# Wider token slots, smaller weight units and one issue order in a fused attention and gated feed-forward kernel

## The chip, the cores and the metric

The kernel runs on one core of a Trainium2 chip. The time is device microseconds from start to end of one execution; 0.5% of it (3.7 us) is about what can be told from no change. Engines: PE (TensorE, matmuls; PEld its weight loads), DVE (VectorE), ACT (ScalarE), POOL (GpSimd) and SP, whose queue issues every DMA. Each engine works its own instructions off in order and waits on semaphores for the others.

## What is computed

```python
# q, k, v: 8 batches x 8 heads x 576 tokens x 64; phi: ... x 32 memories
a = softmax(phi)                                  # over the 32 memories
k_m, v_m = einsum('bhsm,bhsd->bhmd', a, k), einsum('bhsm,bhsd->bhmd', a, v)
attn = softmax(q @ k_m.T / 8)                     # 576 x 32 a head
x = (attn @ v_m) laid out as (4608 tokens, 512)
h = x @ w_in                                      # 512 -> 2048, weights in float64
g = h * clip(h + 3, 0, 6) / 6
out = (g @ w_out).astype(float32)                 # 2048 -> 512, weights in float64
```

## The kernel before

**Folding.** Since x = attn @ v_m, the kernel multiplies v_m into w_in for each batch (the fold, `fold`, L376) and takes the probabilities times that product: h = attn @ (v_m @ w_in). Probabilities, folded weights, gated values and w_out are each split into a high and a low part, and each product is made of three matmuls (high-high, low-high, high-low). The float64 weights arrive as pairs of 32-bit words, and ACT and DVE turn them into float32 in units of 1024 columns (magnitude, rounding, clamp, shift, sign, total); w_in is then kept in DRAM (`w_kept`) and read back for every later batch.

**Slots.** The work after the fold goes in slots: batch b, one block f of 128 of the 2048 hidden columns, and 256 (hf 0) or 320 (hf 1) tokens. A slot is a first GEMM of six matmuls (`gemm1`, L409) into one of two PSUM buffers `ph`, a relu of h + 3 on ACT (L419), a gate on DVE (L423), a high half on ACT (L440), a low half on DVE (L444), and a second GEMM of 2 token tiles x 3 matmuls of 512 columns (`gemm2`, L455) that adds up over all 16 f in a PSUM bank for each token tile. The last 64 tokens of each batch go to a tile `rest`, and two batches' make slots of their own (hf 2). At the end of a run of slots the banks are scaled and stored (`leave`, `store`).

**PSUM.** Four banks for the second GEMM's sums, two for `ph`, and one pair of banks (`psum`, tag pa) that memories, turn, scores and fold take in turn. Each fold makes 512 columns and is drained in two steps of 256 (`folded_high` on ACT, `folded_low` on DVE, L392).

**Attention of a batch.** For batches 0 and 1 the maxima of phi are spread over the partitions by a matmul. From batch 2 on they go through DRAM: `maxima` on DVE from `ptile` (L236), `maxima_out` (L241) writes them to DRAM tensor nmx four bytes at a time, and `spread` (L246) reads them back to every partition as nmxb; then `less_max` on DVE (L261, in three parts), `phi_exp`, `memories` on PE, `turn`, `scores`, and the softmax: transpose, maximum, subtraction on POOL, exponential, sum, division on POOL, transpose back, split. `ptile` and the queries `qh` share a ring of two buffers (`WIDE`).

**Order.** It is written out by hand: BEGIN lists every step word by word up to batch 2, and STEADY says after which slot of a batch each step for the next comes. `play` issues the words in turn, so each engine's queue has its steps in the order of the words. In STEADY the maxima of batch b + 2 come at slot 22 of batch b, their spread at slot 28, and the subtractions with the first slots of the batch after; scores come at slots 8 and 10, and the softmax is spread up to slot 18.

**The words.** pt, pn, kv, q: loads; mx, mo, sp: maxima, their write, their spread; xa, xe: `less_max`, `phi_exp`; kvm, nr, nk, tp, tk: memories up to turned; sc, ct, cm, cs, ex, ds, dr, dm, bt, bh, bl: scores to split probabilities; fo, vh, vl: fold and its two drains; ab, ro, cl, sh, si, to: conversion; g, u, m, k, h, l, a: a slot's first GEMM, relu, gate, rest, high, low, second GEMM; e, eo: `leave`, `store`; fetch, wk: w_in units from and to DRAM.

Of the kernel before, what the change touches and what calls it, by code (L numbers as in the profile page):

```python
# [22 lines left out]
W = (2 * P, S - 2 * P)  # L23
OFF = (0, 2 * P)
REST = S - 4 * P
# [3 lines left out]
NCHUNK = 4  # L29
FC = DF // NCHUNK  # L30
FPC = FC // P
UNIT = 2 * FC
KV = 2 * D + 1
EPS = 1e-9
LAG = 3
VC = 256
VW_RING = {"tag": "vw", "bufs": 6}
TMP = {"tag": "tmp", "bufs": 2}
O_RING = {"tag": "o", "bufs": 2}
# [6 lines left out]

PARTS = ((0, 2), (2, 4), (4, 5))

BEGIN = """
pt.0 raw.0.0 raw.0.1 pn.0 raw.0.2 raw.0.3 kv.0.0 kv.0.1 kv.0.2 mx.0 kv.0.3 md.0 me.0 kv.0.4 ab.0.0.0 ro.0.0.0  # L50
cl.0.0.0 q.0.0 xa.0.0 xa.0.1 xe.0.0 raw2.0 xa.0.2 xe.0.1 sh.0.0.0 xe.0.2 q.0.1 si.0.0.0 ab.0.0.1 ro.0.0.1
raw2.1 cl.0.0.1 kvm.0.0 sh.0.0.1 kvm.0.1 to.0.0.0 kvm.0.2 si.0.0.1 kvm.0.3 kvm.0.4 nr.0 to.0.0.1 nk.0 tp.0 tk.0
sc.0.0 ab.1.0 pt.1 ct.0.0 pn.1 kv.1.0 kv.1.1 kv.1.2 kv.1.3 cm.0.0 fo.0.0 ro.1.0 cl.1.0 kv.1.4 sc.0.1 cs.0.0
sh.1.0 warm.4 ex.0.0 vh.0.0.0 ds.0.0 vh.0.0.1 wk.0 dr.0.0 ab.1.1 dm.0.0 ro.1.1 bt.0.0 q.1.0 mx.1 bh.0.0 raw2.2
ct.0.1 md.1 cm.0.1 q.1.1 me.1 warm.3 vl.0.0.0 cs.0.1 xa.1.0 raw2.3 vl.0.0.1 xe.1.0 xa.1.1 ex.0.1 kvm.1.0 xe.1.1
ds.0.1 kvm.1.1 raw.1.0 si.1.0 kvm.1.2 raw.1.1 xa.1.2 cl.1.1 kvm.1.3 raw.1.2 xe.1.2 dr.0.1 kvm.1.4 sh.1.1 dm.0.1
nr.1 raw.1.3 si.1.1 nk.1 tp.1 raw2.4 tk.1 bl.0.0 sc.1.0 bt.0.1 g.0 ct.1.0 bh.0.1 g.1 to.1.0 raw2.5 u.0 bl.0.1
# [32 lines left out]
bt.2.0 mo.3 ds.2.1 a.56 bh.2.0 m.58 bl.2.0 l.57 h.58 g.60 l.58 u.59 a.57 m.59 u.60 dr.2.1 h.59 m.60 dm.2.1 k.59  # L90
fo.2.0 l.59 h.60 l.60 g.61 bt.2.1 vh.2.0.0 a.58 bh.2.1 vl.2.0.0 vh.2.0.1 bl.2.1 g.62 u.61 vl.2.0.1 a.59 u.62
m.61 m.62 h.61 k.61 l.61 h.62 g.63 l.62 a.60 u.63 m.63 sp.3 q.3.1 h.63 fetch.2.2 a.61 h.64 l.63 k.63 l.64 a.62
h.65 l.65 a.63 e0.62 h.66 e1.62 a.64 l.66 eo.62 h.67 e0.63 e1.63 h.68 a.65 l.67 l.68 h.69 a.66 eo.63 l.69 h.70
a.67 l.70 h.71 a.68 l.71
"""

STEADY = """
0 fold.C.1 un.C.1.0 / 1 un.C.1.1 exps.N.0 / 2 exps.N.1 / 3 exps.N.2 / 5 mem.N / 6 norm.N / 7 turn.N / 8 score.N.0
/ 9 centre.N.0 / 10 exp.N.0 score.N.1 / 11 div.N.0 pt.M / 12 centre.N.1 pn.M / 13 fold.C.2 un.C.2.0 back.N.0 kvs.M
# [7 lines left out]
def attention_ffn_kernel(ctx: ExitStack, tc: tile.TileContext, pn, pt, kv, qt, w1, w2, out):  # L107
# [591 lines left out]
```

## Time and profile before

| | us |
|---|---|
| three runs, median (lowest to highest) | 746.48 (744.11 to 747.0) |
| profiled execution, span from first to last instruction | 744.8 |
| PE busy, of the span | 707.8 (95%) |
| DVE busy | 443.6 (60%) |
| ACT busy | 367.1 (49%) |
| POOL busy | 79.3 (11%) |

The own time of the profiled execution is not given, only its span. Busy shares are means over stages that differ; the slices and windows below show them apart. A busy PE is one with a matmul under way, and matmuls overlap, so the pace is read from the starts of successive groups, not from the length of one.

### The profile page before, as it was taken

The numbers are of one execution on the slowest core, as the hardware profiler recorded it, in microseconds if no ns is written. First come the engines' busy times: TensorE is split into PE (matmuls) and PEld (weight loads), VectorE is DVE, ScalarE is ACT, GpSimd is POOL, SyncE is SP. The second block draws the span as 40 slices with busy tenths as digits, with TensorE's granted clock in tenths as the row PEclk, the third lists the DMA queues.
The fourth block names the chain that finished last, engine by engine and source line by source line (L and its number), as shares of the span: only waits on it lengthen the run. The fifth ranks groups of instructions, "written<-read, shape, count | busy, mean of one in ns | idle before, by whom it ended". The sixth has DMA issues, their size and how long they took to land.

```text
span 744.8 us, 12219 instructions
## 1 busy us (share of the span) xinstructions
PE 707.8 (95%) x4706; PEld 566.8 (76%) x4706; DVE 443.6 (60%) x963; ACT 367.1 (49%) x801; POOL 79.3 (11%) x59
## 2 busy tenths in 40 slices
PE   2859999997999999999999999999999999999997
PEld 1337877875878887888888788788887888888885
DVE  5799999984674464546544465456644465454442
ACT  4457777652454354445444454454443454444442
POOL 0044111120120030003000020002100021000000
PEclk9979999999999999999999999999999999999999
DMA  9991825059940442337251362519081211130002
GB/s 318 370 415 64 292 104 209 1 57 315 367 179 15 186 152 16 141 112 282 8 149 57 111 241 10 147 58 323 15 156 58 73 56 57 58 114 1 1 1 70
DMA packets 26042, 99.77 MB, mean 134 GB/s; under 512 B 4224, under 2 KB 4992, under 8 KB 21376
## 3 DMA queue, kind: packets, MB, share of 16 engines
q1 hardware_dynamic: 25984, 98.99, 41.3%
q8 instruction: 37, 0.61, 0.3%
q14 instruction: 21, 0.17, 0.1%
HBM read 83.25 MB, written 15.73 MB: 133 GB/s over the span
## 4 chain that ended last, share of the span: by engine, by line
PE 81%; DMA 8%; DVE 5%; ACT 3%; issue 3%; SPq 0%; ACTq 0%; DVEq 0%
PE acc L455 49%; PE ph L409 25%; PE pv L376 4%; PE pk L273 2%; DMA ptile<-in_pt 2%; DMA qh<-in_qt 2%; DMA kvt<-in_kv 2%; DMA o<-partial 2%; PE psc L311 1%; ACT gf L419 1%; DVE glo L444 1%; DVE gf L423 1%; DVE pnat L261 1%; DMA raw<-in_w 1%; DVE tmp L161 0%
## 5 line engine op out<-in xcount | busy, mean ns | idle before, releaser
L455 PE MATMUL acc<-w,ghi 128*128 128x512 f32 x1152 | 325.8, 401 | 2.0 <-DVE o L482 1.3
L455 PEld LDWEIGHTS acc<-w,ghi 128*128 128x128 f32 x1152 | 202.8, 189 | 61.1 <-issue 16.4
L419 ACT ACTIVATE gf<-ph,three 128x256 f32<-128x256 f32 (+1 forms) x256 | 127.5, 500 | 166.9 <-PE ph L409 159.0
L423 DVE SCALAR_TENSOR_TENSOR gf<-gf,ph 128x256 f32<-128x256 f32 (+1 forms) x256 | 109.1, 427 | 151.9 <-ACT gf L419 150.7
L409 PEld LDWEIGHTS ph<-phi,both 128*128 128x128 f32 x1024 | 164.7, 190 | 39.0 <-DVE gf L423 12.8
L409 PE MATMUL ph<-phi,both 128*128 128x320 f32 (+1 forms) x1024 | 182.9, 301 | 7.1 <-DVE gf L423 6.7
L455 PE MATMUL acc<-w,glo 128*128 128x512 f32 x576 | 185.2, 397 | 0.0
L440 ACT CAST ghi<-gf 128x256 fp32r<-128x256 f32 x256 | 103.7, 406 | 116.5 <-DVE gf L423 116.3
L444 DVE TENSOR_TENSOR glo<-gf,ghi 128x256 fp32r<-128x256 f32 x256 | 119.8, 470 | 49.9 <-ACT ghi L440 49.5
L455 PEld LDWEIGHTS acc<-w,glo 128*128 128x128 f32 x576 | 108.7, 189 | 25.7 <-DVE glo L444 0.3
L409 PE MATMUL ph<-plo,both 128*128 128x256 f32 (+1 forms) x512 | 110.2, 297 | 0.0
L409 PEld LDWEIGHTS ph<-plo,both 128*128 128x128 f32 x512 | 82.9, 190 | 0.0
L392 DVE TENSOR_TENSOR both<-pv,both 128x512 fp32r<-128x512 f32 x64 | 44.0, 689 | 43.7 <-ACT both L387 43.6
L342 POOL TENSOR_TENSOR st<-st,mx 128x640 f32<-128x640 f32 (+1 forms) x15 | 18.6, 1238 | 372.7 <-DVE mx L338 372.7
L387 ACT CAST both<-pv 128x512 fp32r<-128x512 f32 x64 | 37.1, 583 | 2.6 <-PE pv L376 2.0
L376 PE MATMUL pv<-w,kvT 64*32 64x512 f32 x512 | 36.0, 619 | 0.9 <-DVE st L327 0.9
L273 PE MATMUL pk<-kvt,pnat 128*32 128x129 f32 (+1 forms) x640 | 23.9, 293 | 11.8 <-DMA kvt<-in_kv 8.8
L273 PEld LDWEIGHTS pk<-kvt,pnat 128*32 128x32 f32 (+1 forms) x640 | 17.5, 115 | 18.8 <-ACT raw L149 6.4
L183 POOL TENSOR_TENSOR w<-tmp,w 128x1024 fp32r<-128x1024 f32 x8 | 19.7, 2460 | 81.2 <-ACT w L179 42.4
L367 POOL TENSOR_TENSOR plo<-pT,phi 128x640 fp32r<-128x640 f32 (+1 forms) x15 | 22.4, 1494 | 39.2 <-ACT phi L362 39.2
L354 POOL TENSOR_TENSOR st<-st,sm 128x640 f32<-128x640 f32 (+1 forms) x15 | 18.0, 1202 | 47.6 <-DVE sm L350 47.6
L444 DVE TENSOR_TENSOR glo<-rest,ghi 128x256 fp32r<-128x256 f32 x32 | 13.5, 422 | 15.8 <-PE acc L455 15.8
(56 smaller groups left out, 360.0 us busy)
## 6 DMA issues: line engine op xcount, KB each, us to landing
w<-w_kept SPq DMA_DIRECT2D x24, 1024.0 KB, 8.4
kvt<-in_kv SPq DMA_DIRECT2D x32, 516.0 KB, 8.6
raw<-in_w SPq DMA_DIRECT2D x16, 512.0 KB, 8.7
raw<-in_w SPq DMA_DIRECT2D x8, 1024.0 KB, 14.0
out_t<-o SPq DMA_DIRECT2D x16, 512.0 KB, 2.8
pnat<-in_pn SPq DMA_DIRECT2D x8, 640.0 KB, 6.0
qh<-in_qt SPq DMA_DIRECT2D x8, 640.0 KB, 10.1
ptile<-in_pt SPq DMA_DIRECT2D x8, 576.0 KB, 4.0
```

Of the source, the lines that this page charges most:

```text
L183: nc.gpsimd.tensor_tensor(w2_sb[u][:, 1], whole, w2_sb[u][:, 0].bitcast(F32), ALU.subtract)
L273: nc.tensor.matmul(self.pk[j * M : (j + 1) * M, g, :KV], self.pnat[:rows, t, g * P + j * M : g * P + (j + 1) * M], kvt[:rows, g * NJ + j, ...
L367: self.aux[hf].tensor_tensor(plo, self.pT[hf], probs[self.b, hf][0].bitcast(F32), ALU.subtract)
L376: nc.tensor.matmul(self.pv[c][j * M : (j + 1) * M, g, :], self.kvT[rows, g, j * M : (j + 1) * M], chunk[rows, j, :].bitcast(F32), start=Tr ...
L387: nc.scalar.copy(both[:, 0], self.pv[c][:, :, VC * k : VC * (k + 1)])
L392: nc.vector.tensor_tensor(both[:, 1], src, both[:, 0].bitcast(F32), ALU.subtract)
L409: nc.tensor.matmul(self.ph, w[:, g, fs], x[:, g * n : (g + 1) * n], start=(i == 0), stop=(i == len(seq) - 1),)
L419: nc.scalar.activation(self.gf, self.ph, AF.Relu, bias=three)
L423: nc.vector.scalar_tensor_tensor(gf[:, :n], gf[:, :n], 6.0, ph[:, :n], ALU.min, ALU.mult)
L440: nc.scalar.copy(self.ghi, self.gated())
L444: nc.vector.tensor_tensor(self.glo, self.gated(), self.ghi.bitcast(F32), ALU.subtract)
L455: nc.tensor.matmul(accs[self.b, self.hf][0 if one else k], (self.glo if i == 2 else self.ghi)[:, k * P : (k + 1) * P], w2lo if i == 1 else ...
```

## The change

- Slots take all 576 tokens of a batch for one f: `gemm1` makes 2 x 6 matmuls of 288 columns into a pair of banks, relu and gate are one instruction each over both, the high and low halves take 512 columns, and `gemm2` makes 4 tiles x 3 matmuls. There are 128 slots, 32 for batches 0 and 1 (numbered 0 to 31), then 16 for each batch (96 to 111 are batch 6's).
- The second GEMM of a slot may be issued in quarters (a.95.0 is token tile 0 of slot 95).
- The `ph` buffers and the single pair are replaced by a ring of two pairs (`two_banks`) that first GEMMs, memories, turn, scores and folds share.
- Units of w_in are 256 columns. One word folds one unit, two, or four in a row (two units share a pair of banks); from batch 2 on it is four.
- The halves of scores and softmax are 288 tokens each; the gate of the last 64 tokens goes by way of ACT (`gate_rest`) for every batch; those of two batches make four groups of four f (rh, rl, ra: high, low, second GEMM).
- Loads of batch 1 go to room that later holds parts of w_out. Temporaries, halves and outputs share one ring of six pages.
- BEGIN and STEADY are replaced by ORDER, one list of 1816 words for all engines. `maxima_out` and `spread` are unchanged.

The core of the diff (one stretch of ORDER is shown, from the last slots of batch 5 to the first of batch 6):

```diff
-W = (2 * P, S - 2 * P)
-VC = 256
+HALF = S // 2
+MAIN = 4 * P
+UC = 256
+UNIT = NJ * UC
+PAGE = {"tag": "page", "bufs": 6}
 WIDE = {"tag": "wide", "bufs": 2}
+RUNS = ((0, 0, 6, "keep"), (1, 0, 8, "keep"), (0, 6, 16, "add"), (1, 8, 16, "add"))
...
+ORDER = """
...
+fetch.6.0 k.92 l.90 u.93 m.93 g.94 kv.7.0 k.90 k.93 u.94 h.93 l.93 g.95 a.90 u.95 m.94 m.95 sc.6.0 sc.6.1 a.91 rh.2.1
+h.94 pt.7 ct.6.1 ct.6.0 cm.6.0 fo.6.0.1.2.3 cm.6.1 a.92 a.93 fetch.6.7 cs.6.1 cs.6.0 ex.6.1 mx.7 vh.6.0 ex.6.0 mo.7
+ds.6.1 dr.6.1 q.7.1 vh.6.1 dm.6.1 ds.6.0 fetch.6.4 bt.6.1 sp.7 vh.6.3 dr.6.0 rh.2.2 l.94 h.95 vh.6.2 dm.6.0 l.95 k.95
+a.94 xa.7.0 bh.6.1 kv.7.1 bt.6.0 bh.6.0 xa.7.2 a.95.0 bl.6.1 a.95.1 vl.6.2 rl.2.1 fetch.6.6 a.95.2 fetch.6.5 vl.6.0
+vl.6.1 bl.6.0 rl.2.2 e.7.1 k.94 g.96 a.95.3 vl.6.3 g.97 rh.2.3 u.97 m.97 e.7.3 k.97 u.96 m.96 ra.2.0 g.98 e.7.0 g.99
...
-    ps_h = ctx.enter_context(tc.tile_pool(name="ps_h", bufs=2, space=bass.MemoryType.PSUM))
-    ps_a = ctx.enter_context(tc.tile_pool(name="ps_a", bufs=1, space=bass.MemoryType.PSUM))
+    ps_two = ctx.enter_context(tc.tile_pool(name="ps_two", bufs=2, space=bass.MemoryType.PSUM))
...
+    def two_banks(name):
+        return ps_two.tile([P, 2, 512], F32, name=name, tag="two")
...
+        def fold(self, *units):
+            for u in units:
+                if u == units[0] or len(units) > 2 and u == units[2]:
+                    pair = two_banks("pv")
+                    at = 0
+                self.pv[u] = pair[:, :, at * UC : (at + 1) * UC]
+                at += 1
...
         def gemm1(self):
+            self.ph = two_banks("ph")[:, :, :HALF]
+            for hf in range(2):
+                phi, plo = probs[self.b, hf]
+                seq = [(both[:, k], x, g) for k, x in ((0, phi), (1, phi), (0, plo)) for g in range(NG)]
...
+        def gemm2(self, *tiles):
+            tiles = tiles or range(4)
...
-        play(BEGIN.split())
+        play(ORDER.split())
```

## Rows read from the trace of the kernel before

**Rows 1.** The page's table of engines (all on one line), and its slices: 40 equal parts of the span, busy tenths of PE and of DVE.

```profile
PE 707.8 (95%) x4706; PEld 566.8 (76%) x4706; DVE 443.6 (60%) x963; ACT 367.1 (49%) x801; POOL 79.3 (11%) x59
...
PE   2859999997999999999999999999999999999997
...
DVE  5799999984674464546544465456644465454442
```

**Rows 2.** Windows: busy us of PE, PEld, DVE, ACT and POOL (instructions), granted clock, busy share of the DMA engines, GB/s.

```profile
0.00:20.00 20.00, 5.57 (x66) 3.00 (x66) 10.50 (x19) 7.62 (x12) 0.70 (x6) 1.00 0.92 318
20.00:40.00 20.00, 16.20 (x162) 7.12 (x162) 16.20 (x31) 9.49 (x15) 1.30 (x2) 1.00 1.00 377
40.00:60.00 20.00, 13.21 (x84) 9.18 (x76) 18.26 (x26) 13.46 (x26) 9.98 (x6) 0.74 0.89 365
...
160.00:180.00 20.00, 17.08 (x122) 13.69 (x106) 10.23 (x20) 9.27 (x22) 2.41 (x1) 0.91 0.75 186
180.00:200.00 20.00, 18.69 (x163) 14.43 (x163) 11.94 (x23) 7.08 (x19) 2.00 (x2) 1.00 1.03 374
```

**Rows 3.** Timeline of PE in the steady part: start, us, instructions merged. ph is a first GEMM, acc a second, psc the scores, pv a fold.

```profile
383.18 0.66 PE L409 MATMUL ph<-phi,both 128*128 128x256 f32 x4
...
383.91 1.08 PE L455 MATMUL acc<-w,ghi 128*128 128x512 f32 x4
...
385.30 0.75 PE L409 MATMUL ph<-phi,both 128*128 128x320 f32 x4
...
386.18 1.09 PE L455 MATMUL acc<-w,ghi 128*128 128x512 f32 x4
...
387.58 1.09 PE L455 MATMUL acc<-w,ghi 128*128 128x512 f32 x4
...
421.63 0.66 PE L311 MATMUL psc<-qh,kvT 64*32 64x256 f32 x16
422.22 1.21 PE L455 MATMUL acc<-w,ghi 128*128 128x512 f32 x4
...
434.39 1.09 PE L376 MATMUL pv<-w,kvT 64*32 64x512 f32 x16
435.41 1.19 PE L455 MATMUL acc<-w,ghi 128*128 128x512 f32 x4
```

**Rows 4.** Groups of instructions by form: line, engine, operation, shapes and count, then busy us and mean ns of one, and the idle time before them.

```profile
L444 DVE TENSOR_TENSOR glo<-gf,ghi 128x256 fp32r<-128x256 f32 x256 | 119.8, 470 | 49.9 <-ACT ghi L440 49.5
...
L440 ACT CAST ghi<-gf 128x256 fp32r<-128x256 f32 x256 | 103.7, 406 | 116.5 <-DVE gf L423 116.3
...
L423 DVE SCALAR_TENSOR_TENSOR gf<-gf,ph 128x256 f32<-128x256 f32 x224 | 93.9, 419 | 147.6 <-ACT gf L419 146.6
...
L419 ACT ACTIVATE gf<-ph,three 128x320 f32<-128x320 f32 x128 | 67.4, 527 | 94.0 <-PE ph L409 90.8 <-DVE glo L444 2.6 <-ACT raw L149 0.5
L419 ACT ACTIVATE gf<-ph,three 128x256 f32<-128x256 f32 x128 | 60.5, 473 | 72.9 <-PE ph L409 68.2 <-DVE glo L444 4.0 <-ACT both L387 0.2
...
L392 DVE TENSOR_TENSOR both<-pv,both 128x512 fp32r<-128x512 f32 x64 | 44.0, 689 | 43.7 <-ACT both L387 43.6
...
L423 DVE SCALAR_TENSOR_TENSOR gf<-gf,ph 128x320 f32<-128x320 f32 x32 | 15.4, 482 | 4.3 <-ACT gf L419 4.0
...
L236 DVE TENSOR_REDUCE nmx<-ptile 128x2 f32<-128x1152 f32 x8 | 10.7, 1342 | 4.3 <-DMA ptile<-in_pt 4.3
```

**Rows 5.** The DMA view: issues by tensor, count, KB each, median us from issue to landing; then the last line of the view of the write of nmx (L241), and that of the view of the tile nmxb.

```profile
ptile<-in_pt SPq DMA_DIRECT2D x8, 576.0 KB, 4.0
...
out_t<-o SPq DMA_DIRECT2D x8, 128.0 KB, 2.3
...
DMA to landing us min/median/max: 6.8/8.6/9.0
...
DMA to landing us min/median/max: 4.0/6.6/6.8
```

**Rows 6.** Timelines of SP, DVE and PE where batch 2's phi maxima pass through DRAM, and a window just after (columns as in rows 2).

```profile
156.06 0.38 SPq L241 DMA_DIRECT2D nmx<-nmx  x1
...
164.06 0.32 SPq L246 DMA_DIRECT2D nmxb<-nmx  x1
...
170.97 1.63 DVE L261 TENSOR_TENSOR pnat<-pnat,nmxb 128x512 f32<-128x512 f32 x3 [3.78 <-DMA nmxb<-nmx]
...
172.46 0.65 PE L273 MATMUL pk<-kvt,pnat 128*32 128x129 f32 x16 [2.92 <-ACT pnat L265]
...
174.00:178.00 4.00, 4.00 (x16) 3.40 (x15) 1.39 (x4) 1.48 (x5) 0.00 (x0) 0.59 1.06 230
```

**Rows 7.** Timelines of POOL and DVE at the same time in the front: a low half of w_out on POOL, and a slot's low half on DVE.

```profile
49.68 2.36 POOL L183 TENSOR_TENSOR w<-tmp,w 128x1024 fp32r<-128x1024 f32 x1 [3.37 <-ACT w L179]
...
49.94 2.38 DVE L444 TENSOR_TENSOR glo<-gf,ghi 128x256 fp32r<-128x256 f32 x1 [0.49 <-ACT ghi L440]
```

**Rows 8.** Timeline of PE in the front: the first slot, the wait after it, and the start of the stretch without breaks.

```profile
44.16 1.22 PE L409 MATMUL ph<-phi,both 128*128 128x256 f32 x4
...
53.90 0.82 PE L409 MATMUL ph<-phi,both 128*128 128x256 f32 x4 [4.55 <-DVE gf L423]
...
57.51 0.90 PE L409 MATMUL ph<-phi,both 128*128 128x320 f32 x4
```

**Rows 9.** Timeline of PE: its last matmuls.

```profile
739.61 0.62 PE L455 MATMUL acc<-w,glo 128*128 128x512 f32 x2
```

More of the change, by code (lines that the diff above doesn't have):

```diff
@@ L22 @@
 NT = 5
[L23 to L25 removed]
+HALF = S // 2
+MAIN = 4 * P
+REST = S - MAIN
 NG = 2
@@ L90 @@
[L90 to L98, printed above, removed]
@@ L254, in every @@
         def every(self):
-            self.nmx = bank()[:, : NG * P]
+            self.nmx = two_banks("nmxb")[:, 0, : NG * P]
             nc.tensor.matmul(self.nmx, ones, self.diag, start=True, stop=True)
@@ new lines, in low @@
+        def low(self):
+            nc.vector.tensor_tensor(self.parts[:, 1], self.gf[:, :MAIN], self.parts[:, 0].bitcast(F32), ALU.subtract)
+        def gemm2(self, *tiles):
+            tiles = tiles or range(4)
+            w2hi, w2lo = w2_parts(self.f)
+            for i, (k, w) in enumerate(((0, w2hi), (0, w2lo), (1, w2hi))):
+                for t in tiles:
+                    if self.first and i == 0:
+                        accs[self.run, t] = bank()
+                    nc.tensor.matmul(
+                        accs[self.run, t],
+                        self.parts[:, k, t * P : (t + 1) * P],
+                        w,
+                        start=self.first and i == 0,
+                        stop=self.last and i == 2,
+                    )
@@ L444, in low @@
-            nc.vector.tensor_tensor(self.glo, self.gated(), self.ghi.bitcast(F32), ALU.subtract)
+            nc.vector.tensor_tensor(self.parts[:, 1], self.gated(), self.parts[:, 0].bitcast(F32), ALU.subtract)
         def gemm2(self):
-            one = self.hf == 2
-            if self.first:
-                accs[self.b, self.hf] = [bank() for _ in range(1 if one else 2)]
-            order = [(k, i) for i in range(3) for k in range(2)]
-            if self.last and not one:
-                order.sort()
@@ L453, in gemm2 @@
-            for n, (k, i) in enumerate(order):
-                w2hi, w2lo = w2_parts(self.f + (k if one else 0))
-                nc.tensor.matmul(
-                    accs[self.b, self.hf][0 if one else k],
-                    (self.glo if i == 2 else self.ghi)[:, k * P : (k + 1) * P],
-                    w2lo if i == 1 else w2hi,
-                    start=self.first and (n == 0 if one else i == 0),
-                    stop=self.last and (n == len(order) - 1 if one else i == 2),
-                )
@@ L502, in attention_ffn_kernel @@
-    accs, outs, partial, waiting = {}, {}, {}, {}
-    def recall(b, hf):
-        waiting[b, hf] = sb.tile([P, 2, DM], F32, name="o", **O_RING)
-        nc.sync.dma_start(out=waiting[b, hf], in_=partial[b, hf])
-    def pairs(fs):
-        return [(hf, f) for f in fs for hf in range(2)]
-    def halves(fs):
-        return [(hf, f) for hf in range(2) for f in fs]
-    slots, starts = [], []
-    def segment(b, order, kind="out"):
-        starts.append(len(slots))
-        fs = {hf: [f for h, f in order if h == hf] for hf in range(3)}
-        slots.extend(Slot(b, hf, f, f == fs[hf][0], f == fs[hf][-1], kind) for hf, f in order)
@@ L532, in warm @@
+    slots, runs = [], []
+    for run, (b, lo, hi, kind) in enumerate([*RUNS, *((b, 0, NFT, "out") for b in range(2, B))]):
+        runs.append((b, kind))
+        slots.extend(Slot(run, b, f, f == lo, f == hi - 1) for f in range(lo, hi))
+    rests = [[Rest(p, r) for r in range(4)] for p in range(B // 2)]
     def warm(n):
@@ L618, in table @@
-    def table(text, start):
-        rows = {}
-        for line in text.split("/"):
-            words_ = line.split()
-            if words_:
-                rows.setdefault(start + int(words_[0]), []).extend(words_[1:])
-        return rows
     with tc.manual_schedule():
```

518 lines of the change are left out of this document (242 added, 276 removed), and 3 rows, old and new, of the table GROUPS.

## The prediction

> **What bounds the kernel now.** I read the page's table of engines first: TensorE (PE) is busy 707.8 of 744.8 us, VectorE (DVE) 443.6, ScalarE (ACT) 367.1 [rows 1]. The slices below it, and then the 20 us windows, say that this is a mean over two different stretches. After 200 us PE has no idle time to speak of. Before that, PE is busy 5.6, 16.2 and 13.2 us of the first three windows, and 17.1 and 18.7 of the two from 160 to 200 [rows 1, 2]. DVE is the other way round: 16.2, 18.3 us in the second and third window, and its slices stay at 8 to 9 tenths until about 160 us, then drop to about half. So up to 160 us DVE converts weights and sets the pace, and afterwards PE does. A gain has to come from PE's idle time before 200 us, from PE's own work, or not at all; and any wait that appears on PE after 200 us is added to the time in full, because nothing there is slack.
>
> **PE's own work hardly changes.** In the steady part a 256-token first GEMM (six matmuls) takes 383.91 - 383.18 = 0.73 us and a 320-token one 386.18 - 385.30 = 0.88; a second GEMM of two token tiles takes 387.58 - 386.18 = 1.40 [rows 3]. Per block f of 128 hidden columns that is 0.73 + 0.88 = 1.61 and 2 x 1.40 = 2.80 us. The new slot has the same six times 576 columns in as many matmuls (12 of 288), and the same 12 matmuls of 512: again 1.61 and 2.80, change 0. For the fold: 512 columns take 435.41 - 434.39 = 1.02 us, and the scores, which use the array in the same 64x32 tiles, take 422.22 - 421.63 = 0.59 for 256 [rows 3]. So 0.43 us is 256 columns' streaming and 0.16 is paid once per burst. Two folds of 512 were 2.04 us; a burst of four units is between 4 x 0.43 + 0.16 = 1.88 (the fixed part paid once) and 4 x 0.59 = 2.36 (each time). I take 1.9 to 2.1 since the units follow each other in one queue. With 12 such bursts, 8 lone units (0.59 each) and 4 pairs in batches 0 and 1 instead of 8 folds, and the two halves of the scores in one burst (8 x 0.16 saved), I take -2 us, bounds -4 and +4.
>
> **ACT and DVE get fewer, longer instructions.** From 256 to 320 columns the relu grows from 473 to 527 ns and the gate from 419 to 482, about 0.85 and 1 ns a column; so 576 columns cost some 740 ns on either. The split's two halves at 512 columns cost about 0.62 (ACT) and 0.69 to 0.74 us (DVE, [rows 4]). DVE per f in batches 0 and 1: 0.42 + 0.48 + 2 x 0.47 = 1.84 before, 1.45 after, 0.39 less, 12 us over 32 f. After 200 us this is worth nothing: PE's 4.4 us per f covers it before and after.
>
> **The front, up to 160 us.** The first 576-token slot needs both halves' probabilities, so the whole softmax of batch 0, where now 256 tokens are enough. Now the first slot starts at 44.16, PE waits 4.55 us for the gate at 53.90, and runs without a break from 57.5 [rows 8]. Read off the new order, DVE has 22 steps (some 16 us by [rows 4] and their like) between the end of batch 0's memories and the last low half of its probabilities, and the first transfer is now a 1 MB weight unit, 2.8 us at the 377 GB/s of the second window [rows 2]: first slot near 42 us, but the next ones wait on DVE for weight units that the new order converts earlier (nine by the eighth slot). The 12 us of DVE time saved help here and only here. Against it works GpSimd (POOL): its 2.36 us instruction at 49.68 held a 0.47 us DVE subtract until 52.3 [rows 7], and the new order leaves as many POOL instructions in this stretch. The Trainium skill, SBUF - State Buffer, section Who interferes with whom, says the same as an exclusive lock: a DVE instruction with two SBUF inputs and a GpSimd one that reads SBUF block each other whole; the trace agrees with 2.38 us for that subtract. I take -1.5 us for the front, bounds -10 (most of the 12 us reaches PE) and +8 (PE starves on conversions until 90 us).
>
> **Start of batch 2, 160 to 200 us.** Here PE idles 2.9 + 1.3 us [rows 2], and its clock is at 0.59 over 174 to 178, which costs 4 x 0.41 = 1.6 us [rows 6]. What happened is a lesson for the rest: the phi maxima go out to DRAM at 156.06 (nmx), their broadcast (nmxb) could only be issued at 164.06, and DVE's subtract that needs it sat until 170.97, 14.9 us after the first issue, with PE idle behind it until 172.46. The new order puts several f of matmuls between; a wait of about 1.5 us for the recalled partial sums stays likely. 5.8 - 1.4 = 4.4 us gained, bounds 0 and 5.8.
>
> **The turns from batch to batch.** This term decides. The code of the maxima's two transfers is unchanged: nmx lands 6.8 to 9.0 us after issue (median 8.6), nmxb 4.0 to 6.8 (median 6.6), ptile at a median of 4.0 [rows 5]. Now the attention of the next batch is spread over some twenty slots and DVE's phi subtractions come more than ten slots after the maxima. In the new order scores, fold and softmax stand in one block just ahead of the batch's first slot, and DVE, which is in order, has the subtractions for the batch after that (xa) in the same block. ptile's buffer ring has two places, both held by the queries until the scores have read them, so the chain can't start before sc. For batch 6, from the start of sc.6.0: scores 0.8, ptile 4.0, maxima 1.35 [rows 4], nmx 8.6, nmxb 6.6; xa.7.0 can start at 21.4. Behind it on DVE wait the transpose bt.6.0 (0.8 with xa's 0.7 ahead of it), a short xa (0.4), and vl.6.2, rl.2.1 and vl.6.0 (0.69 each), without which g.96 can't finish its third matmul: 25.4 us. PE has queued ahead of g.96: scores 1.3, four second GEMMs 11.2, the fold burst 2.1, three quarters of a fifth 2.1, together 16.7. PE stands 8.7 us, or 4.3 with the smallest landings. In the same way batch 5: maxima end at about 10.8 (behind softmax work), xa.6.2 at 25, then 1.1 and the gate m.80 0.75 = 26.9, and g.82 wants the PSUM pair at 22.0: 4.9 (1.7 to 6.2). Batch 3: vl.3.1 behind three xa, 1.5 (0 to 4.1). Batch 2: e.3 and m.33 behind xa.3.2, 1.9 (0 to 2). Batch 4 has xa behind the gates that matter, 0; batch 7 has no successor. Sum 17.0, and one clock drop like that of 174 us, 1.6: +18.6, bounds 6 and 24. SP too is in order: behind sp.7's wait for nmx stand kv.7.1 and three weight fetches, with over 10 us of slack on PE, so nothing.
>
> **The end.** After the last matmuls at 739.61 [rows 9] come one eviction and a store, as before: 0, within 1 us.
>
> **The sum.** The profiled span is 744.8; its execution's own time isn't given, and the median of the three runs is 746.5, 1.7 above the span. 744.8 - 2 - 1.5 - 4.4 + 18.6 + 0 = 755.5, and 1.7 around it: **757 us**.
>
> **Rivals.** (1) The turns are hidden: the subtractions' data is there when DVE comes to them, that is when nmx and nmxb together take under some 7 us in batch 6 (9 in batch 5). Place and price: the 18.6 us above go, 757.2 - 18.6 = **738.6**, faster. For it: DVE's queue reaches xa.7.0 only some 13 us after sc.6.0, an error of a few us in my reading of either queue shrinks the wait, and the extra DVE time could lengthen PE's lead. Against: none of the six nmx landed under 6.8 us. (1a) The same result by another mechanism: if both transfers landed as fast as the 128 KB stores, 2.3 us each [rows 5], xa.7.0 could start at 0.8 + 4.0 + 1.35 + 2 x 2.3 = 10.8 us, before DVE comes to it, and all turns would be hidden: 738.6 again. Six of six landings of nmx speak against it; of rival 1's chance I give it 0.03. The Trainium skill, DMA: Bandwidth & Descriptors, section Anatomy of one DMA, states a rule of this kind, a fixed cost of about 2.0 us plus the bytes over 436 GB/s. The trace disagrees, with 8.6 and 6.6 us.
>
> (2) Half and half: smallest landings and the shorter waits at the turns (8 us with the clock), **747**, no change that can be measured.
>
> (3) DVE in the front is worse than I take: with +8 instead of -1.5 the time is **767**. For it: the collisions of [rows 7]; against: 12 us less DVE work.
>
> (4) The change doesn't do what it says: the queues could be filled in another order than the text's words. The order of the old text's words stands in the old trace, so I give it no share of its own.
>
> **Chances.** Forecast (750 to 764) 0.49; hidden turns 0.31; half and half 0.14; front 0.06. A difference of 0.5%, 3.7 us, is about what can be told from no change here. Faster: 0.31 and 0.02 of the half case, 0.33; within: 0.12; slower: 0.49 + 0.06 = 0.55. The likeliest case alone reaches from 750 (bounds of the turns at 10) to 764. The range for 8 in 10 has to take in most of rival 1 with a front that gains a little more, and most of rival 3: 734 to 768.
>
> **What would show it.** Right: PE waits of 4 to 9 us ahead of g.96 and of 3 to 6 ahead of g.82, each with a DVE phi subtraction waiting for nmxb just before it and a lower clock behind it; nmx still landing after 7 to 9 us; second GEMM 1.40 per two tiles, four-unit fold about 2 us. Wrong: PE busy without a break from 200 us to the end (rival 1), or PE under 15 us of 20 in the windows from 60 to 100 (rival 3). If the fold burst takes over 2.4 us or the first slot starts after 50 us, those steps fail.

## The result and the profile after

The kernel after takes 751.21 us (median of 7 runs, 748.15 to 754.99); 7 runs of the kernel before beside it have a median of 746.48. The ratio is 1.0073, 95% interval 1.0047 to 1.0099: slower by 0.7%, where 757 was forecast. The profiled execution has a span of 748.9 us and a time of 750.7.

The page's table of engines, and its slices of PE, of DVE and of PE's clock, which answer to [rows 1]:

```profile
PE 690.6 (92%) x5204; PEld 577.5 (77%) x5204; DVE 401.0 (54%) x596; ACT 321.3 (43%) x623; POOL 81.2 (11%) x59
...
PE   1578899999998999899999999799986999999996
...
DVE  5989989864645336543455345443445424634231
...
PEclk9889999999999999999999999899997999999999
```

DVE and ACT each have over 40 us less work, fewer and longer instructions as forecast, and the time is longer all the same. After 200 us (slice 10) PE, which had no gap in [rows 1], now has them, the largest about 480 and 560 us, where batches 5 and 6 begin, and behind both its clock falls.

Windows (columns as in [rows 2]) of the front, of the start of batch 2, and of the turn to batch 5:

```profile
0.00:20.00 20.00, 4.49 (x50) 2.42 (x50) 12.28 (x17) 10.62 (x15) 3.47 (x7) 1.00 0.93 339
20.00:40.00 20.00, 12.12 (x180) 6.57 (x180) 19.49 (x35) 7.97 (x14) 3.74 (x3) 0.83 0.93 318
40.00:60.00 20.00, 15.13 (x137) 11.21 (x130) 17.48 (x25) 12.78 (x22) 5.29 (x3) 0.91 0.84 315
160.00:180.00 20.00, 20.00 (x139) 17.19 (x138) 9.85 (x15) 6.65 (x15) 1.06 (x1) 1.00 0.38 132
180.00:200.00 20.00, 20.00 (x202) 16.49 (x201) 9.57 (x16) 7.39 (x17) 1.58 (x2) 1.00 0.68 235
474.00:490.00 16.00, 11.18 (x56) 10.35 (x55) 7.29 (x12) 7.56 (x17) 0.00 (x0) 0.79 0.57 192
```

The turn to batch 6, in the timelines of SP, DVE and PE. It answers to [rows 6] and is read in the order of time: ptile is loaded, the maxima go out (nmx) and come back to every partition (nmxb), DVE's phi subtraction gets them, and PE gets its first slot (g.96):

```profile
543.41 0.33 SPq L244 DMA_DIRECT2D ptile<-in_pt  x1
...
548.95 0.38 SPq L278 DMA_DIRECT2D nmx<-nmx  x1
...
556.89 0.32 SPq L283 DMA_DIRECT2D nmxb<-nmx  x1
...
563.23 0.69 DVE L298 TENSOR_TENSOR pnat<-pnat,nmxb 128x512 f32<-128x512 f32 x1 [8.52 <-DMA nmxb<-nmx]
...
568.69 1.30 PE L438 MATMUL ph<-phi,both 128*128 128x288 f32 x4 [9.60 <-DVE both L422]
```

PE's releaser here is the drain of a fold on DVE (both, L422), but that drain stood in DVE's queue behind a subtraction that had waited 8.52 us for a DMA. The chain from the first load to that subtraction is 19.8 us long, and 14.3 of it are the two small transfers. The other turns, DVE's line and then PE's for batches 5, 3 and 2:

```profile
479.01 1.03 DVE L298 TENSOR_TENSOR pnat<-pnat,nmxb 128x256 f32<-128x256 f32 x2 [7.15 <-DMA nmxb<-nmx]
480.76 1.33 PE L438 MATMUL ph<-phi,both 128*128 128x288 f32 x4 [4.82 <-DVE gf L454]
...
304.99 1.63 DVE L298 TENSOR_TENSOR pnat<-pnat,nmxb 128x512 f32<-128x512 f32 x3 [3.89 <-DMA nmxb<-nmx]
307.27 0.80 PE L438 MATMUL ph<-phi,both 128*128 128x288 f32 x4 [2.01 <-DVE both L422]
...
223.34 0.43 DVE L298 TENSOR_TENSOR pnat<-pnat,nmxb 128x256 f32<-128x256 f32 x1 [4.30 <-DMA nmxb<-nmx]
227.49 1.33 PE L438 MATMUL ph<-phi,both 128*128 128x288 f32 x4 [2.12 <-DVE gf L454]
```

The view of waits sums them (us, times, longest):

```profile
DVE pnat L298 <- DMA nmxb<-nmx: 25.7, 5, 8.5
...
PE ph L438 <- DVE both L422: 13.5, 5, 9.6
...
PE ph L438 <- DVE gf L454: 7.9, 3, 4.8
```

To set the two profiles against each other term by term, I priced the matmuls that are still to come at 160 us and at 200 us, in both kernels, at the mean step from one start to the next that each kind has in the kernel before from 240 to 700 us, with steps that a wait had lengthened left out (288 columns at the mean of 256 and 320, a fold of 256 at half of one of 512). At 160 us 560.5 us of work are left before and 560.6 after, at 200 us 528.6 and 520.8. A loss behind 200 us is a step that took longer than its kind's mean.

| term of the sum | forecast | measured |
|---|---|---|
| front, to 160 us | -1.5 | +0.1 |
| start of batch 2, 160 to 200 us | -4.4 | -7.9 |
| turns, after 200 us: the waits, and the lower clock behind them | +18.6 | +25.3 |
| other small losses after 200 us | not in the sum | -5.2 (11.0 before, 5.8 after) |
| PE's own work after 200 us | -2 | -9.0 |
| tail | 0 | +1.1 |
| span | +10.7 | +4.1 |

The measured terms add up to +4.4; the 0.3 left over is what the prices miss.

### The profile page after: what moved, and what is told of

Read it like the earlier page. It is cut to its first block, busy times and chain, and to the rows that moved or that the text cites. A ratio compares the mean times of both kernels' runs of the same rounds, so it can differ in the third digit from the quotient of the medians.

```text
span 748.9 us, 12439 instructions
## 1 busy us (share of the span) xinstructions
PE 690.6 (92%) x5204; PEld 577.5 (77%) x5204; DVE 401.0 (54%) x596; ACT 321.3 (43%) x623; POOL 81.2 (11%) x59
## 4 chain that ended last, share of the span: by engine, by line
PE 76%; DVE 11%; DMA 9%; issue 2%; ACT 1%; SPq 0%; DVEq 0%; ACTq 0%
PE acc L474 39%; PE ph L438 25%; PE acc L530 6%; DMA nmx<-nmx 3%; PE pv L407 3%; PE pk L310 2%; DMA nmxb<-nmx 2%; DVE tmp L202 2%; DMA ptile<-in_pt 1%; DMA qh<-in_qt 1%; PE psc L343 1%; DVE pnat L298 1%; DVE gf L454 1%; DMA o<-partial 1%; DVE nmx L273 1%
## 5 line engine op out<-in xcount | busy, mean ns | idle before, releaser
L474 PE MATMUL acc<-w,parts 128*128 128x512 f32 x1536 | 375.0, 394 | 0.0
L474 PEld LDWEIGHTS acc<-w,parts 128*128 128x128 f32 x1536 | 282.8, 189 | 65.4 <-issue 8.0
L438 PE MATMUL ph<-phi,both 128*128 128x288 f32 x1024 | 185.2, 304 | 21.4 <-DVE both L422 13.5
L454 DVE SCALAR_TENSOR_TENSOR gf<-gf,ph 128x576 f32<-128x576 f32 x128 | 95.5, 753 | 176.9 <-ACT gf L451 176.8
L451 ACT ACTIVATE gf<-ph,three 128x576 f32<-128x576 f32 x128 | 94.4, 742 | 177.5 <-PE ph L438 148.1
L465 DVE TENSOR_TENSOR parts<-gf,parts 128x512 fp32r<-128x512 f32 x128 | 96.5, 761 | 40.3 <-ACT parts L462 39.4
L438 PE MATMUL ph<-plo,both 128*128 128x288 f32 x512 | 111.7, 300 | 0.0
L462 ACT CAST parts<-gf 128x512 fp32r<-128x512 f32 x128 | 79.0, 622 | 61.2 <-DVE gf L454 43.2
L422 DVE TENSOR_TENSOR both<-pv,both 128x512 fp32r<-128x512 f32 x64 | 42.3, 681 | 30.9 <-ACT both L418 30.8
L530 PE MATMUL acc<-w,parts 128*128 128x512 f32 x192 | 45.7, 390 | 0.1
L530 PEld LDWEIGHTS acc<-w,parts 128*128 128x128 f32 x192 | 35.6, 188 | 7.7 <-DVE o L498 0.5
L407 PE MATMUL pv<-w,kvT 64*32 64x256 f32 x1024 | 34.1, 384 | 7.7 <-DVE pnat L298 3.5
L458 ACT COPY rest<-gf 128x64 f32<-128x64 f32 x128 | 30.4, 245 | 9.6 <-DVE gf L454 9.5
L298 DVE TENSOR_TENSOR pnat<-pnat,nmxb 128x512 f32<-128x512 f32 (+1 forms) x24 | 13.6, 593 | 27.1 <-DMA nmxb<-nmx 25.7
```

What stands on the lines that cost most here:

```text
L407: nc.tensor.matmul(self.pv[u][j * M : (j + 1) * M, g], self.kvT[rows, g, j * M : (j + 1) * M], chunk[rows, j, :].bitcast(F32), start=True, ...
L422: nc.vector.tensor_tensor(both[:, 1], self.pv[u], both[:, 0].bitcast(F32), ALU.subtract)
L438: nc.tensor.matmul(self.ph[:, hf], w[:, g, fs], x[:, g * HALF : (g + 1) * HALF], start=(i == 0), stop=(i == len(seq) - 1),)
L451: nc.scalar.activation(self.halves(), self.ph, AF.Relu, bias=three)
L454: nc.vector.scalar_tensor_tensor(self.halves(), self.halves(), 6.0, self.ph, ALU.min, ALU.mult)
L458: nc.scalar.copy(rest[:, self.f, at : at + REST], self.gf[:, MAIN:])
```

## The experiments

Queue theory, the prediction's: VectorE works in order, and a phi subtraction at its head that waits for nmxb holds everything behind it. Rival, the pair theory: a turn is as long as its chain of softmax, fold and two shared PSUM pairs, and the wait is only one of several that end together. Ratios are to runs of the kernel before on the same chip.

| run | median us | ratio, 95% interval |
|---|---|---|
| e1_phi_later | 737.01 | 0.987 (0.985 to 0.989) |
| e2_rows_of_8_bytes | 736.20 | 0.987 (0.986 to 0.989) |
| e3_before_late_max | 764.38 | 1.025 (1.024 to 1.026) |
| e6_before_early_max2 | 739.53 | 0.992 (0.991 to 0.993) |
| e5_rows8_phi_later | 729.56 | 0.978 (0.977 to 0.979) |
| e8_two_writes | 732.99, one run | - |
| e4_front | 742.11 | 0.995 (0.993 to 0.996) |
| e7_front_again | 740.98 | 0.993 (0.991 to 0.995) |
| e10_front_pad32 | 740.56 | 0.993 (0.992 to 0.994) |
| e11_remedies_pad32 | 736.81 | 0.988 (0.987 to 0.990) |
| e12_before_pad32 | 744.07 | 0.997 (0.996 to 0.998) |
| e13_front_pad992 | 734.92 | 0.986 (0.983 to 0.988) |

**Phi subtractions later.** The words move in ORDER, and nothing else (batches 3 and 7 shown; batch 6's go behind m.82, and vl.3.1 ahead of xa.4.0):

```diff
-g.34 xa.3.2 xe.3.2 rc.3.1
+g.34 rc.3.1
...
-m.36 k.36 l.34 h.36
+m.36 k.36 l.34 xa.3.2 xe.3.2 xa.3.1 xe.3.1 xa.3.0 xe.3.0 h.36
...
-a.94 xa.7.0 bh.6.1 kv.7.1 bt.6.0 bh.6.0 xa.7.2 a.95.0
+a.94 bh.6.1 kv.7.1 bt.6.0 bh.6.0 a.95.0
...
-l.98 rl.2.3 a.96.0 xa.7.1
+l.98 rl.2.3 xa.7.2 xe.7.2 xa.7.0 a.96.0 xa.7.1
```

> The kernel after with nothing but places in the issue order changed: the phi subtractions of batches 3, 6 and 7, with their exponentials, are issued some two to four slots later, behind the gate and the low part of slots 34, 82 and 98, and the low part of one fold of batch 3 ahead of batch 4's. Queue theory (the prediction's): VectorE works in order and stands in a phi subtraction for nmxb, which lands some 15 us after the maxima, and the gates and low parts queued behind it starve TensorE; so the waits of 9.6, 4.8 and 2.1 us ahead of g.96, g.82 and at batch 3's phi go, with the 2.9 us of lower clock behind one of them and 2.0 us at batch 4's: about -20 us, 725 to 737 us, ratio 0.97 to 0.99. Pair theory (rival): a turn between batches lasts as long as its chain of softmax, fold and two shared PSUM pairs, and the wait on nmxb is only the first of several that end at about the same time; then the next one takes its place, 745 to 752 us, ratio 0.998 to 1.008.

Measured 737.01, at the upper end of the range, 14 us under the kernel after, and below the kernel before. The wait on nmxb falls from 25.7 us in five places to this line of the view of waits:

```profile
DVE pnat L299 <- DMA nmxb<-nmx: 5.1, 2, 2.6
```

No other wait of that size takes its place, so the pair theory falls. Of the 20 us expected 6 are missing in the median: PE still loses 2.2 and 1.8 us at 225 and 237 us and some 3 at 482 to 487.

**The same data sooner.** The places stay, the write changes:

```diff
-            self.row = dram.tile([NG, P], F32, name=f"nmx{self.b}")
-            nc.sync.dma_start(out=self.row.rearrange("g p -> p g"), in_=self.nmx)
+            self.row = dram.tile([P, NG], F32, name=f"nmx{self.b}")
+            nc.sync.dma_start(out=self.row, in_=self.nmx)
...
+            part = part.rearrange("p n (g q) -> p n g q", g=NG)
+            nmx = self.nmx.rearrange("p (q g) -> p g q", g=NG).unsqueeze(1)
```

> The kernel after, with the negated maxima written to DRAM as 128 rows of two numbers (128 pieces of 8 bytes in place of 256 of 4) and read back in that order by the phi subtraction. Queue theory: each microsecond by which the landing of the small write falls below the 7.1 us median of the kernel after comes off the VectorE stalls of four turns, so about 4 us of time for 1 us of landing; at an unchanged landing the time stays at 751. Pair theory: 748 to 754 us whatever the landing.

Measured 736.20, 15 us less. The DMA view of the kernel after, then that of this one:

```profile
nmx<-nmx SPq DMA_DIRECT2D x6, 1.0 KB, 8.3
```

```profile
nmx<-nmx SPq DMA_DIRECT2D x6, 1.0 KB, 3.6
```

So the write lands 4.7 us sooner and the time falls by 15, some 3 us for each; 4 were expected. (The 7.1 us of the expectation is the median of the write and the read back taken together; the write alone had 8.3.) One stall, ahead of g.96, is left: there nmxb needed 7.7 us from its issue at 542.00 to DVE's start at 549.67.

```profile
555.12 1.30 PE L443 MATMUL ph<-phi,both 128*128 128x288 f32 x4 [7.26 <-DVE both L427]
```

**The same fault put into the kernel before.**

```diff
-/ 20 fold.C.3 un.C.3.0 / 21 un.C.3.1 / 22 max.M / 24 fetch.N.1 / 27 fold.N.0 un.N.0.0 / 28 un.N.0.1 spread.M
-/ 29 fetch.N.2 q.M.1
+/ 20 fold.C.3 un.C.3.0 / 21 un.C.3.1 / 24 fetch.N.1 / 27 fold.N.0 un.N.0.0 / 28 un.N.0.1
+/ 29 fetch.N.2 q.M.1 / 31 max.M spread.M
```

> The kernel before with one thing moved: the maxima of the batch after next and both small transfers are issued at slot 31 of a batch in place of slots 22 and 28, with nothing else changed. Queue theory: the phi subtractions of batches 4 and 6, which come one to three slots after the turn, then wait some 9 us on VectorE for nmxb, TensorE loses 5 to 8 us at each; batches 5 and 7 have eight slots of rest between and lose 0 to 1 each: +10 to +17 us, 756 to 763 us, ratio 1.013 to 1.023. Pair theory: the kernel before has no shared pairs and slots of 256 and 320 tokens, so the same wait costs nothing there that the queues don't take up: 745 to 749 us, ratio 0.998 to 1.004.

Measured 764.38, 18.6 us more, just over the range. The timelines of DVE and PE at one of the two turns without rest slots:

```profile
321.57 0.69 DVE L261 TENSOR_TENSOR pnat<-pnat,nmxb 128x512 f32<-128x512 f32 x1 [7.67 <-DMA nmxb<-nmx]
...
323.25 2.07 PE L455 MATMUL acc<-w,ghi 128*128 128x512 f32 x4 [7.69 <-DVE o L486]
```

The other such turn loses 7.72 us in the same way, the clock is at 0.66 and 0.57 in the 5 us behind them, where some 2 us more are lost at each, and batches 5 and 7 wait for nothing. Wide slots and shared pairs aren't needed for the loss.

**And the kernel before without its own fault.** Batch 2's words move in BEGIN:

```diff
-fo.1.2 mx.2 u.42 a.40 m.42 mo.2 wk.3
+fo.1.2 u.42 a.40 m.42 wk.3
...
-l.34 u.36
+l.34 mx.2 mo.2 u.36
...
-l.38 u.39
+l.38 sp.2 u.39
...
-h.45 sp.2 k.45
+h.45 k.45
```

> The kernel before with one thing moved: batch 2's maxima and its small write are issued behind the low part of slot 34 and the read back behind that of slot 38, about ten slots earlier than before; its phi subtractions stay where they are. Queue theory: the wait on nmxb at 172.46 us and the low clock behind it go, -4 to -6 us: 740 to 743 us, ratio 0.992 to 0.995. If the gain of the kernel after between 160 and 200 us comes from its longer slots and folds instead, 745 to 748 us, ratio 0.998 to 1.002.

Measured 739.53, 6 us less. Its windows (as [rows 2, 6]) have no gap and full clock:

```profile
160.00:180.00 20.00, 20.00 (x172) 16.14 (x171) 12.67 (x27) 10.71 (x27) 2.40 (x1) 1.00 0.58 219
180.00:200.00 20.00, 20.00 (x133) 16.17 (x131) 15.11 (x29) 9.72 (x24) 4.79 (x5) 1.00 0.83 308
174.00:178.00 4.00, 4.00 (x60) 3.06 (x60) 3.21 (x6) 1.08 (x3) 0.00 (x0) 1.00 0.49 189
```

What the kernel after gains from 160 to 200 us is thus for the most part (6.4 of 7.9 us by lost PE time) the same wait, which its order doesn't have.

**Both remedies together**, the two edits above in one kernel.

> Both remedies at once: the small write as 128 rows of 8 bytes, and the phi subtractions of batches 3, 6 and 7 later. Queue theory: of the 13 to 15 us that each gives alone most is the same stalls, but each leaves some: the first leaves a stall of 7.4 us ahead of g.96, the second about 7 us in three places; with both none of them is left, 726 to 732 us, ratio 0.973 to 0.981, below both kernels. Pair theory: at 735 to 738 a turn has come to what the pairs and the softmax chain allow, and nothing more is to be had, ratio 0.986 to 0.989.

Measured 729.56, 2.2% under the kernel before. In its view of waits no phi subtraction waits for nmxb, and PE's first GEMM waits for DVE in these two lines:

```profile
PE ph L444 <- DVE gf L460: 4.1, 4, 1.2
...
PE ph L444 <- DVE both L428: 1.9, 3, 1.3
```

A variant asks why the small write was slow:

```diff
-            nc.sync.dma_start(out=self.row, in_=self.nmx)
+            for g in range(NG):
+                nc.sync.dma_start(out=self.row[:, g : g + 1], in_=self.nmx[:, g : g + 1])
```

> The kernel with both remedies, its small write split into two of 128 pieces of 4 bytes. The write of 256 pieces of 4 bytes took 8.3 us in the median to land, that of 128 pieces of 8 bytes 3.6. If the number of pieces makes it slow, each of the two lands in 3 to 5 us; if pieces of 4 bytes do, in 7 to 9. Time: within 4 us of the kernel with both remedies, since few stalls are left for it to lengthen.

Its DMA view:

```profile
nmx<-nmx SPq DMA_DIRECT2D x12, 0.5 KB, 7.0
```

Two such writes follow each other, the second issued some 0.4 us behind the first. The first of each pair, 128 pieces like the write of 8 bytes but half the bytes, landed after 10.5, 3.6, 6.4, 6.1, 7.9 and 5.9 us in batches 2 to 7, the 8-byte write in e5 after 7.8, 3.5, 4.0, 3.0, 3.5 and 5.3: in five of six the 4-byte pieces took 0.6 to 4.4 us longer. By the two landings expected, 3 to 5 us if the number of pieces decided and 7 to 9 if their size did, the 7.0 speaks for the size. It isn't shown: this is one profiled run, and the second write, in the queue before the first had landed, can have held the first up, so that 256 pieces were again on their way together. The Trainium skill, DMA: Bandwidth & Descriptors, section Anatomy of one DMA, puts most of a small DMA's fixed 2 us on the confirmation that the last byte has landed, which it says can be surprisingly long into HBM. It says so of DMAs that GpSimd issues, while all of these, the prediction's too, are issued by SP. The runs agree in that the bytes don't decide, since half of them took longer; the size and the number of the pieces are not in that rule.

**The front, twice.** The first try (batch 0's phi, maxima and values ahead of the 1 MB of raw2.0):

```diff
-raw2.0 ab.1.0 cl.1.0 pt.0 sh.1.0 raw.0.0 pn.0 raw.0.1 ro.1.0 mx.0 ab.0.0 ro.0.0 md.0 me.0 xa.0.0
+pt.0 raw.0.0 pn.0 mx.0 md.0 me.0 raw.0.1 ab.0.0 ro.0.0 xa.0.0
...
-kv.0.4 pt.1 sx.0 xe.0.2 q.0.1 si.0.1 kvm.0.3
+kv.0.4 raw2.0 ab.1.0 ro.1.0 pt.1 xe.0.2 q.0.1 si.0.1 cl.1.0 sh.1.0 si.1.0 to.1.0 kvm.0.3
```

> The last kernel, with the front changed as well: the 1 MB of the first piece of the second weight matrix, which the kernel after loads first of all, is loaded behind the five value tiles of batch 0, its arithmetic is issued behind that of the first two units of the first matrix, and batch 0's maxima come ahead of it. If the front is late (first slot at 40.12 us, first matmul at 10.07 against 6.70) because these 1 MB stand ahead of batch 0's phi and values in the one transfer queue, values land 2.4 us earlier and the time falls by 1.5 to 2.5 us against the last kernel. If VectorE, busy without a gap from 11 to 46 us, sets the front, its work is only moved and the time stays within 1 us or gets worse by up to 2.

742.11, 12.5 us worse than e5, which neither theory had. Its timelines of PE and ACT show the values 2.5 us earlier than the 16.02 of the kernel after, and then what the edit had overlooked: ACT too is in order, and the exponential that PE needs (xe.0.2, L308) now stood behind work on a late transfer:

```profile
13.52 2.28 PE L316 MATMUL pk<-kvt,pnat 128*32 128x129 f32 x32 [5.64 <-DMA kvt<-in_kv]
...
24.19 1.08 PE L316 MATMUL pk<-kvt,pnat 64*32 64x129 f32 x16 [4.72 <-ACT pnat L308]
...
21.69 1.12 ACT L187 ACTIVATE tmp<-raw 128x1024 f32<-128x1024 f32 x1 [8.37 <-DMA raw<-in_w]
```

The second try, against the first, clears that queue:

```diff
-kv.0.4 raw2.0 ab.1.0 ro.1.0 pt.1 xe.0.2 q.0.1 si.0.1 cl.1.0 sh.1.0 si.1.0 to.1.0 kvm.0.3
+kv.0.4 q.0.1 q.0.0 pt.1 raw2.0 xe.0.2 si.0.1 kvm.0.3
...
-to.0.1 tk.0 sx.0
+to.0.1 tk.0 ab.1.0 ro.1.0
...
-bl.0.1 nr.1 q.1.1
+bl.0.1 nr.1 cl.1.0 sh.1.0 si.1.0 to.1.0 q.1.1
```

> The kernel with both remedies (729.6 us, ratio 0.978) and the front changed once more. In the first try at the front the values did land 2.5 us earlier (first value matmul at 13.52 against 16.02 us), but ScalarE stood 8.4 us for the 1 MB piece that had been moved back, with the last phi exponential of batch 0 queued behind it. Here that piece's first two ScalarE operations come behind the turned memory of batch 0, its VectorE work behind batch 1's weights, its split behind slot 0's high part. If transfers set the front, the first slot begins near 37 us in place of 40, and the time falls by 1.5 to 3 us against the kernel with both remedies, ratio 0.974 to 0.976; if VectorE sets it, the 3.9 us of moved VectorE work come back before 130 us and the time is the same within 1 us, ratio 0.977 to 0.980.

740.98, still 11.4 us worse than e5. The scores start 3.2 us earlier than there (22.80 against 25.99 us), but the first slot at 40.63 against 40.57, so the gain is used up in between; that VectorE and the steps of batch 1 behind it take it is argued, not shown. By the work left at 160 us it is 3.6 us worse than e5 up to there. Of the rest only some 0.5 us is a wait.

**Where matmuls of the same form differ.** Twelve matmuls of the second GEMM, one line each from the timelines of e5 and then of e7, both at full clock:

```profile
606.22 2.88 PE L480 MATMUL acc<-w,parts 128*128 128x512 f32 x12
```

```profile
605.02 2.96 PE L480 MATMUL acc<-w,parts 128*128 128x512 f32 x12
```

From 240 to 700 us one follows the other after 230 to 231 ns in the mean in e5 and in the kernel after, 235 in both tries at the front; the first GEMM's step is 133 ns in e5 and in the second try alike. What differs is where the tiles lie in SBUF. No trace shows addresses; I worked them out from the kernels' text, with the tiles of a pool laid out in the order of their first use. The stationary tiles (parts) are pages of one ring. In e5 and the kernel after that ring comes first, and they lie a whole multiple of 4096 bytes from the second weight matrix, since all that stands between are tiles of such a size. In the tries five tiles come ahead of it, 9216 + 24576 + 5120 + 32 + 1024 = 39968 bytes a partition, 992 short of ten times 4096. The edit for three kernels is one tile that nothing reads, ahead of all working tiles:

```diff
+        pad = sb.tile([P, 1], F32, name="pad", tag="pad", bufs=1)
+        nc.vector.memset(pad, 0.0)
```

> The kernel of the second try at the front with a tile of 4 bytes a partition, which nothing reads, allocated (and zeroed once) ahead of all other working tiles, so that these lie 32 bytes further on and the weights stay where they were. In both tries at the front each matmul of the second GEMM came 235 ns after the one before it (mean, 240 to 700 us), in the kernel with both remedies 230, in the kernel before 238; moving the first loads had also moved the stationary tiles of the second GEMM in SBUF, to 0 bytes past a multiple of 64, as they lie in the kernel before; in the kernel after they lie 32 past it, as the second weight matrix does in all. Address theory: with 32 bytes of pad the interval is 230 again and the time 5 to 8 us lower than the 741.0 us, 733 to 736 us, ratio 0.982 to 0.986. If the order of the work at the front makes those matmuls slow, nothing changes: 740 to 742, ratio 0.991 to 0.995.

> The kernel with both remedies and the same 32 bytes of pad: its stationary tiles come to a multiple of 64 bytes. Address theory: the interval goes from 230 to 235 ns, 1536 matmuls by 5 ns are 7 us, 735 to 738 us, ratio 0.985 to 0.990. Otherwise 729 to 731 us, ratio 0.976 to 0.980.

> The kernel before with the same 32 bytes of pad: its stationary tiles of the second GEMM come to 32 bytes past a multiple of 64, where those of the kernel after lie. Address theory: the second GEMM's interval falls from 238 to some 232 ns and the time by 5 to 10 us, 737 to 742 us, ratio 0.988 to 0.994; then that much of the kernel after's gain in TensorE's own work is no merit of its longer slots. Otherwise 745 to 748 us, ratio 0.998 to 1.002.

32 bytes cost the kernel with both remedies 7.2 us (736.81), at an interval of 235 ns. So the place of the tiles is enough: all the pad does is to move every working tile by 32 bytes and to add one memset at the start, and the first GEMM's step stays at 133 ns. But the same pad didn't mend the second try (740.56), and the kernel before gained only 1.2 to 2 us, so the offset within 64 bytes, as I had put it, is not the rule. With 248 in place of 1 in the pad the distance is a multiple of 4096 again:

> The kernel of the second try at the front with a pad of 992 bytes in place of 32. A pad of 32 bytes slowed the second GEMM of the kernel with both remedies from 230 to 235 ns a matmul and its time by 7 us, yet the same pad mended neither this kernel nor, by more than 1 us, the kernel before. In the kernel after and in that with both remedies the stationary tiles lie a whole multiple of 4096 bytes behind the second weight matrix in SBUF; here, with 992 bytes, they do so again. If that distance is what counts, the interval is 230 ns and the time falls by 5 to 8 us from 740.6 to 741.0, 733 to 736 us, ratio 0.982 to 0.986. If not, 740 to 742 us, ratio 0.991 to 0.995.

734.92: 6 us back, the interval at 231 ns. Of the 5 us that it stays above e5, some 3 are lost PE time before 160 us. The second weight matrix has the same place in all these kernels, so the runs don't tell whether the distance counts, or the stationary tiles' own place. The timelines of e11 and then of e13:

```profile
604.80 2.95 PE L480 MATMUL acc<-w,parts 128*128 128x512 f32 x12
```

```profile
605.01 2.91 PE L480 MATMUL acc<-w,parts 128*128 128x512 f32 x12
```

## Why the prediction was right, step by step

**The turns** carried it, and their mechanism is shown: e1 and e2 take the wait away by two unlike means, and e3 makes it in the kernel before. Forecast for batches 6, 5, 3 and 2: 8.7, 4.9, 1.5, 1.9; measured 9.60, 4.82, 2.01, 2.12, batch 4 nothing, in sum 18.6 for 17.0 (19.2 by the steps of the table). What was sized too small is the clock: 1.6 us was allowed in all, and behind the waits of batches 2, 5 and 6 the lower clock cost 1.6, 2.8 and 1.6; behind batch 3's it stayed at full speed, and 0.2 was lost. Windows behind the waits of batches 6, 5, 2 and 3, in this order (the granted clock is the third number from the end; 1.00 is 2.4 GHz, and the lower of the two levels, 1.2 GHz, is 0.50):

```profile
568.60:572.60 4.00, 3.91 (x15) 3.78 (x16) 1.74 (x3) 0.00 (x0) 0.00 (x0) 0.55 0.02 4
480.70:487.00 6.30, 6.24 (x24) 5.95 (x25) 3.76 (x7) 4.24 (x10) 0.00 (x0) 0.51 0.65 259
227.40:231.40 4.00, 3.91 (x18) 3.91 (x19) 2.51 (x5) 1.01 (x3) 0.00 (x0) 0.57 0.94 289
307.20:311.20 4.00, 3.93 (x27) 3.81 (x28) 2.13 (x4) 2.75 (x6) 0.00 (x0) 1.00 1.01 245
```

So the term came to 25.3, just past its upper bound of 24. That the time is 6 us under the forecast all the same, and not above it, comes from three other terms: the start of batch 2 gained 3.5 us more, PE's own work 7 more, and 5.2 came from small losses that the sum put at nothing, since I took the kernel before as without slack after 200 us. It loses 11.0 us there, in pieces of 0.1 to 1.1 per 20 us, and the kernel after 5.8. That errors of up to 7 us in single terms leave the sum only 6 us off is luck; that the waits come, at which batches and for how long, is not. Rival 1 (738.6) fell; against rival 1a's 2.3 us none of the six writes of nmx landed under 7.3. Half and half (747) fell too.

**Start of batch 2:** forecast -4.4, measured -7.9. The wait of about 1.5 us for recalled sums, which I held to be likely, didn't come (window 160 to 200: PE 20.00 of 20 twice), and the mechanism was that of [rows 6], as e6 shows.

**The front:** forecast -1.5, measured +0.1, inside its bounds. The first slot came at 40.12 us, earlier than the 42 forecast, and the wait of 4.55 us in [rows 8] is gone: PE loses 5.5 us less from 40 to 60 us. But the first matmul comes at 10.07 (6.70 before), and from 80 to 140 us PE loses 3.9 us more, most of it in waits for DVE of 1.81, 0.92 and 1.01 us at 82.60, 112.95 and 128.51 us. Rival 3 (767) didn't happen. Whether another order could win here stays open: both of mine lost.

**PE's own work:** forecast -2, measured -9.0, outside the bounds of -4 and +4. Lines from PE's timeline in the kernel after:

```profile
533.86 2.88 PE L474 MATMUL acc<-w,parts 128*128 128x512 f32 x12
536.58 0.70 PE L438 MATMUL ph<-phi,both 128*128 128x288 f32 x4
...
546.66 1.96 PE L407 MATMUL pv<-w,kvT 64*32 64x256 f32 x64
548.55 10.54 PE L474 MATMUL acc<-w,parts 128*128 128x512 f32 x45
```

The fold of four units took 548.55 - 546.66 = 1.89 us (1.88 to 2.36 allowed). The step that failed is "the same 12 matmuls of 512: change 0": twelve took 2.75 us from start to start (median of 50; 2.72 above), not 2.80, which is 4.2 ns a matmul and 5.8 us over the 1387 matmuls after 200 us; the fold gave 1.8 of the rest, scores 0.8, the first GEMM 0.6. That the place of the tiles matters at this size is shown by e11 and e13; that it explains the difference between the two kernels is only argued, since e12 tried one distance. With e11's 7 us on it the kernel after would stand at 758, an estimate from that run.

**The tail:** 0 forecast, +1.1 measured, just over the 1 us allowed: from the last matmul's end to the end of the span it is 4.6 us before and 5.7 after.

**What the change is worth without the fault.** With the nmxb waits out of both, the kernels stand at ratios 0.978 (e5) and 0.992 (e6), some 10 us apart; with the slower addresses (e11) at 0.988, some 3 us apart.

## What to carry to other kernels

Where a short chain goes through DRAM, add up its landings from the trace and set them against the place of its first reader in an in-order queue; that sum forecast each wait at a turn here to within 1 us, and moving the reader or shortening the landing was worth 2%. When a new order moves a load, list what stands behind its first user on every engine (e4). And before an edit is credited with some per cent of TensorE's time, compare the interval between equal matmuls: an allocation that moved can be the cause.

## What the hardware showed that I had not expected

- A DMA to DRAM of 256 pieces of 4 bytes landed 8.3 us after issue (median), of 128 pieces of 4 bytes, issued in pairs, 7.0, of 128 pieces of 8 bytes 3.6.
- Equal matmuls of the second GEMM follow each other after 230 or 235 ns (means of e5 and e11), by where the stationary tiles lie in SBUF. By the places worked out above it is 230 to 231 where they lie a whole multiple of 4096 bytes from the moving ones, and 235 at 32 bytes more, at 992 less and at 960 less. Whether the distance counts or the tiles' own place, why, and which smaller step would do, stays open.
